# An mLSTM kernel with a feed-forward block: first weight quarter loaded first and converted between the first two cells, no warm-up matmuls, k scaled where v was

## The chip, the core and the metric

The kernel runs on one core of a Trainium2 chip. Its time is the device time of one execution in microseconds (us); the figure before the change is the median of three executions. The profile is that of one further execution. Engines are named as in the profile: PE (matrix engine; PEld is its loading of stationary operands), DVE (vector engine), ACT (scalar engine), POOL (GpSimd), SP (the sync engine, which here only issues DMAs). An engine's name with a q behind it, as SPq or ACTq, is its instruction queue, where DMAs are issued.

## The reference

Two blocks follow one another. The first is an mLSTM cell over 4 batches x 8 heads, 768 time steps, head dimension 40. The second takes its output as 3072 tokens of 320 features through a feed-forward block of width 2048 with a leaky ReLU.

```
for t in range(S):
    m_new = max(f[t] + m, i[t])
    f_stab, i_stab = exp(f[t] + m - m_new), exp(i[t] - m_new)
    C = f_stab * C + i_stab * outer(v[t], k[t])
    n = f_stab * n + i_stab * k[t]
    denom = max(|n . q[t]|, 1)
    y[t] = sigmoid(o[t]) * (C @ q[t]) / denom
x = y as (4*768, 320)
h = x @ w_in                       # 320 x 2048
out = max(0.01 * h, h) @ w_out     # 2048 x 320
```

q, k, v and the gates are 4-byte floats. The two weight matrices arrive as 8-byte floats and are made into 4-byte floats inside the kernel.

## The kernel before

**Chunks and cells.** Time is cut into NB = 6 chunks of 128 steps. A cell is one chunk of one batch, with all 8 heads: 24 cells, numbered s = 4c + b. Inside a cell the recurrence is written as products: scores k·q, a weight matrix from the gates, values from weights and v, and a state handed to the next chunk. Chunk 0 has no state before it and is handled by code of its own; later chunks work on two halves of 64 steps.

**Gates.** `gates(c)` makes running sums and maxima of the gates on DVE, `gates_exp(c)` their exponentials on ACT, `gates_T(c)` transposes them on PE (the result, `gT`, is copied by DVE). For c = 0 the gates lie in `f0` and `i0`, tiles of 128 rows that hold RG copies of the 32 (batch, head) rows. For c > 0, `gates_exp` also writes two results to DRAM (`a_dr`), from where SP spreads them over partitions (`spread`, `spread_q`).

**A cell of chunk 0.** `spread_mask(s)` (L411) puts a causal mask into PSUM with PE, `spread_first(s)` (L422) adds gate sums to it with narrow matmuls, `prep_exp` (L439) takes eight exponentials on ACT into the tile `w`. `u_transpose` (L514, L517) transposes k and q on PE and copies them to `kqT` on ACT. `u_scores` (L526) makes k·q on PE and multiplies it into `w` on DVE (L530). `prep_vu` (L449, L453) multiplies v with a gate on POOL. `u_state` (L538, L546) makes the state from k and that scaled v. `u_values` (L613) multiplies `w` with v. `prep_o` and `gate` (L467, L604 to L628) apply the output gate on ACT, DVE and POOL, and `u_x` (L719 to L724) transposes the cell's result into `xT`, the input of the feed-forward block.

**A cell of a later chunk.** `prep_mask` (L430) adds the mask on POOL, `prep_state` scales the state on POOL (L558) and calls `prep_vu`, which here scales v half by half in two POOL operations (L460). `u_parts` makes scores (L584) and the state's increment (L589) on PE, DVE multiplies and adds (L594, L562), `prep_kq` scales q on DVE (L486). `u_plain` (chunk 1) or `u_mix` (later ones) makes the outputs. `prepare_step(n)` fills constant parts of the state tile of slot n with three memsets on POOL (L156 to L158); there are NL = 4 slots.

**Weights.** `w_in` comes in QN = 4 quarters of 512 columns. `load_weights(n)` issues a quarter as ten DMAs of 128 KB, 64 partitions each (L213); `w_out` comes in 8 pieces of one DMA (L218). `narrow_weights(n)` is a Python generator of seven steps that converts one piece from 8 to 4 bytes: an Abs on ACT (L231), then six operations on DVE (L233, L237, L241, L243, L245, L247). Each call of `next` puts one step into the program at that place. A quarter's steps work on 128 x 1280 elements.

**Feed-forward.** `ff_units(0)` gives the units of chunk 0: each of the first 16 is a half unit, 20 records on PE (L734) followed by two leaky ReLUs on ACT (L742); the rest are the second product (L769). Later chunks have units of their own. A cell's output of chunk c is fed to the feed-forward units of chunk c while the cells of chunk c + 1 run.

**What sets the order.** PE, DVE, ACT and POOL run in the order in which the Python program emits their instructions (`manual_schedule`). For the first chunk this order is written out by hand in `first_chunk`. After it comes a loop over c: for c = 1 it goes through the remaining 30 feed-forward units of chunk 0, emits some steps of weight conversion before each (`run(now, ...)`), and puts in a cell's part wherever `place` says (the list holds a unit number for each of 13 parts). SP's queue is ordered by the tile framework and runs in order as well; a DMA on SP or ACT waits for the one that used the same of 8 completion semaphores before.

**Buffers.** The masks of a cell, and each feed-forward unit, take two of the four PSUM buffers of the pool `psf`; transposes, scores, values and states share four of the pool `psc`.

Of the kernel before, what the change touches and what calls it, by code (L numbers as in the profile page):

```python
# [9 lines left out]
F32 = mybir.dt.float32  # L10
# [3 lines left out]
ALU = mybir.AluOpType  # L14
# [4 lines left out]
def kernel(  # L19
# [58 lines left out]
    dr = ctx.enter_context(tc.tile_pool(name="dr", bufs=1, space=bass.MemoryType.DRAM))  # L78


    RG = P // BH
    f_all = f_gate.rearrange("b h s -> (b h) s")
    i_all = i_gate.rearrange("b h s -> (b h) s")
    f0 = gp.tile([P, P], F32, name="f0")
# [5 lines left out]

    def load_fi(c):
        t = fi[c] = wk.tile([BH, 2, P], F32, name="fi")
        eng = nc.scalar if c < 3 else nc.sync
        eng.dma_start(t[:, 0, :], f_all[:, ts(c, P)])
        eng.dma_start(t[:, 1, :], i_all[:, ts(c, P)])

    load_fi(1)
    load_fi(2)

    ident = consts.tile([P, P], F32, name="ident")  # L100
    make_identity(nc, ident[:])
# [86 lines left out]
    def load_weights(n):  # L188

        m = n - QN  # L190
        if n < QN:
            dst = w_in[:, n, :]
        else:
            dst = w_out[:, 2 * m : 2 * m + 2, :].rearrange("p a d -> p (a d)")
        to = dst
        if wide:
            if n < 2:
                at = NF * GT - 2 * WC * (n + 1)
                raw = acts_l[:, at : at + 2 * WC].bitcast(U64)
            elif n < QN:  # L200
                raw = raw_t[:, WC * (n - 2) : WC * (n - 1)]
            elif m < 2:
                raw = w_out[:].rearrange("p f d -> p (f d)")[:, (2 + m) * WC : (3 + m) * WC].bitcast(U64)
            else:
                at = (4, 0, 1, 2, 3, 4)[m - 2] * HW
                raw = raw_t[:, at : at + HW]
            raws[n] = (raw, dst)
            to = raw
        if n < QN:
            src = moe_w_in[:, n * QC : (n + 1) * QC].rearrange("(k p) (r c) -> r p k c", p=DP, r=2)  # L210
            for slot in range(KC):
                for r in range(2):
                    nc.sync.dma_start(  # L213
                        to[DP * r : DP * (r + 1), 2 * P * slot : 2 * P * (slot + 1)], src[r, :, SLOTS[r][slot], :],
                    )
        else:
            rows = moe_w_out[2 * m * P : 2 * (m + 1) * P, :]
            nc.sync.dma_start(to.rearrange("p (a d) -> p a d", d=Dm), rows.rearrange("(a p) d -> p a d", p=P))  # L218
# [37 lines left out]
    def gates(c):  # L256


        m0 = m0s.get(c)
        n = P if c == 0 else BH  # L260
        fc, il = (f0[:], i0[:]) if c == 0 else (fi[c][:, 0, :], fi[c][:, 1, :])
        F = wk.tile([n, P], F32, name="F", bufs=1)
        nc.vector.tensor_tensor_scan(F[:], fc, zeros[:n].to_broadcast([n, P]), 0.0, op0=ALU.add, op1=ALU.add)
        if c > 0:
            il_t = wk.tile([BH, P], F32, name="il", bufs=1)
            nc.vector.tensor_scalar(il_t[:], il, scalar1=m0[:], scalar2=None, op0=ALU.subtract)
            il = il_t[:]
        m = wk.tile([n, P], F32, name="m", bufs=1)
        nc.vector.tensor_tensor_scan(m[:], fc, il, -1e30 if c == 0 else 0.0, op0=ALU.add, op1=ALU.max)
        a = f0 if c == 0 else wk.tile([n, P], F32, name="a", bufs=1)  # L270
        nc.vector.tensor_tensor(a[:], F[:], m[:], op=ALU.subtract)
        bu = wk.tile([BH, 3, P], F32, name="bu", bufs=1)
        nc.vector.tensor_tensor(bu[:, 0, :], il[:BH], F[:BH], op=ALU.subtract)
        if c + 1 < NB:
            m1 = wk.tile([BH, 1], F32, name="m0")
            if c == 0:
                nc.vector.tensor_copy(m1[:], m[:BH, P - 1 :])
            else:
                nc.vector.tensor_tensor(m1[:], m0[:], m[:, P - 1 :], op=ALU.add)
            m0s[c + 1] = m1  # L280
        if c > 0:
            na = wk.tile([BH, 1], F32, name="na")
            nc.vector.tensor_tensor(na[:], m[:, SL - 1 : SL], F[:, SL - 1 : SL], op=ALU.subtract)
        bus[c] = bu, a, (na if c > 0 else None)
# [156 lines left out]
    def prep_vu(s):  # L441

        c, b = divmod(s, B)
        d = st[s]
        if s < NS:
            d["vu"] = wk.tile([P, H, 2, V1], F32, name="vu")
            g = gT[c][:, 1, ts(b, H)].unsqueeze(2).unsqueeze(3)
            if c == 0:
                nc.gpsimd.tensor_tensor(  # L449
                    d["vu"][:, :, :, :DB], d["va"][:, :, :D].rearrange("p h (k d) -> p h k d", d=DB),  # L450
                    g.to_broadcast([P, H, 2, DB]), op=ALU.mult,
                )
                nc.gpsimd.tensor_tensor(  # L453
                    d["vu"][:, :, :, DB], d["va"][:, :, D : D + 2], gT[c][:, 1, ts(b, H)].unsqueeze(2).to_broadcast([P, H, 2]),
                    op=ALU.mult,
                )
            else:
                for u in range(2 if c + 1 < NB else 1):
                    rows = ts(u, SL)
                    nc.gpsimd.tensor_tensor(  # L460
                        d["vu"][rows], S_v[s % NL][rows, u, :, :, :V1], g[rows].to_broadcast([SL, H, 2, V1]), op=ALU.mult,
                    )

    def prep_o(s):

# [104 lines left out]
    def u_parts(s):  # L570
# [11 lines left out]
        for h in range(H):  # L582
            for u, toks, rows in subs(s):
                nc.tensor.matmul(  # L584
                    bank[1 - u][toks, h, :], lhsT=kqT[rows, 0, ts(h, SL)], rhs=kqT[rows, 1, ts(h, SL)], start=True, stop=True,
                )
            for u, toks, rows in subs(s):
                if u < ends:
                    nc.tensor.matmul(  # L589
                        dC[u][:, h].rearrange("p k d -> p (k d)"), lhsT=d["k"][toks, h, :D],  # L590
                        rhs=d["vu"][toks, h].rearrange("p k d -> p (k d)"), start=True, stop=True,
                    )
        for u, toks, rows in subs(s):
            nc.vector.tensor_tensor(mixed(s)[toks, u], w[toks], bank[1 - u][toks], op=ALU.mult)  # L594
# [208 lines left out]
    def run(steps, n=None):  # L803

        for _ in range(H if n is None else n):
            next(steps, None)
# [18 lines left out]

    def first_chunk():

        load(0)
        load(1)
        load_o(0)  # L830
        load_o(1)
        load_weights(0)
        load(2)
        load(3)
        load_o(2)
        load_o(3)
        gates(0)
        gates_exp(0)
        warm(6)
        spread_mask(0)  # L840
        spread_mask(1)
        u_transpose(0)
        bu, a, _ = bus[0]
        gates_T(0, bu)
        spread_first(0, a)
        run(prep_exp(0))
        spread_first(1, a)
        prep_vu(0)
        prep_vu(1)
        prepare_tiles()  # L850
        u_transpose(1)
        u_scores(0)
        u_state(0)
        run(prep_exp(1))
        gates(1)
        gates_exp(1)
        load_weights(1)
        u_scores(1)
        u_values(0)
        u_state(1)  # L860
        spread_mask(2)
        spread_first(2, a)
        prep_o(0)
        gate(0)
        prep_o(1)
        spread_mask(3)
        spread_first(3, a)
        u_values(1)
        gate(1)
        w = narrow_weights(0)  # L870
        for _ in range(2):
            next(w, None)
        u_x(0)
        u_transpose(2)
        run(prep_exp(2))
        prep_vu(2)
        u_x(1)
        for _ in w:
            pass
        u_transpose(3)  # L880
        prep_vu(3)
        u_scores(2)
        u_state(2)
        run(prep_exp(3))
        prepare_step(0)
        prepare_step(1)
        ffs = ff_units(0)
        ffs[0]()
        ffs[1]()
        u_scores(3)  # L890
        u_values(2)
        u_state(3)
        prep_o(2)
        gate(2)
        w = narrow_weights(1)
        next(w, None)
        u_gates(1)
        u_values(3)
        prep_o(3)
        gate(3)  # L900
        u_x(2)
        for _ in w:
            pass
        u_x(3)
        prepare_step(2)
        prepare_step(3)
        return ffs

    E = mybir.EngineType
    with tc.manual_schedule(engines={E.PE, E.DVE, E.Activation, E.Pool}):  # L910
# [12 lines left out]

        ffs = ffs[2:]
        fetch = {4: (3, 4), 8: (5, 6), 13: (7,)}
        place = (5, 7, 9, 11, 11, 13, 15, 17, 20, 21, 23, 25, 27)
        now = (None for n in range(2, QN + NF // 2) for _ in narrow_weights(n))
        for c in range(1, NB + 1):
            if c > 1:
# [5 lines left out]
            for i in range(n_ff):  # L935
                if c == 1:
                    run(now, 2 if i < 10 else 3 if i < 14 else 4)
                    for n in fetch.get(i, ()):
                        load_weights(QN + n)
                    if i == 3:  # L940
                        prep_mask(B)
                        prep_state(B)
                        ahead(B)
                        load_fi(3)
# [59 lines left out]
```

## Time and profile before

| | us |
|---|---|
| median of 3 executions | 543.99 (543.73 to 547.78) |
| the profiled execution | 544.61 |
| its span in the trace | 542.8 |
| PE busy | 523.8 (97%) |
| DVE busy | 245.2 (45%) |
| ACT busy | 156.5 (29%) |
| POOL busy | 127.5 (23%) |

The largest groups of PE are the two products of the feed-forward block: L734 219.9 us and L769 215.1 us. The page's chain of waits, followed back from the last instruction, is PE for 81% of the span, DVE for 9%, SP's queue for 5%. Busy shares are means over the whole span; the page also cuts the span into 40 slices of 13.6 us and gives each engine's busy share in each slice as a digit of tenths. The row PEclk is the clock that PE was granted, in tenths of full speed. In the timeline the first two numbers of a row are start and length in us; brackets at the end hold the idle time before the first instruction of the row, and what ended it. A matmul of 4-byte floats shows as two records.

### The profile page before, as it was taken

To read this page: it belongs to the slowest core of one execution; us is meant where nothing else is said; L and a number is where in the kernel's file an instruction comes from. 1 tells how busy PE (TensorE), PEld (TensorE's weight loads), DVE (VectorE), ACT (ScalarE), POOL (GpSimd) and SP (SyncE) were. 2 spreads that over 40 slices of the span, in tenths; PEclk is the share of its full clock that TensorE was granted. 3 is DMA by queue.
4 is the path that set the end of the run, shared out by engine and by line. 5 is a ranking of instruction groups with operands and counts; after the bars stand their busy time and mean duration, and the time that the engine had idled before them with its cause. 6 is when DMAs were issued, how large, how long until landed. Compare 5 with 4: busy or idle time off the path is not lost.

```text
span 542.8 us, 11533 instructions
## 1 busy us (share of the span) xinstructions
PE 523.8 (97%) x4572; PEld 335.7 (62%) x4572; DVE 245.2 (45%) x423; ACT 156.5 (29%) x426; POOL 127.5 (23%) x157
## 2 busy tenths in 40 slices
PE   8978887989999999999999999999999999999997
PEld 7768776756745567645477644577654577644675
DVE  2659999999326445235536135525035532000000
ACT  4544735442233312034221034320043400022100
POOL 4346424351203332203332103323002200000000
PEclk9978999998999999999999999999999999999999
DMA  9967787876424655554556645555532121100000
GB/s 127 168 177 168 167 187 202 190 170 146 105 55 111 132 129 124 156 111 105 127 138 131 145 104 108 121 141 139 134 98 57 45 83 35 46 0 1 12 13 24
DMA packets 166005, 60.21 MB, mean 111 GB/s; under 512 B 129024, under 2 KB 156224, under 8 KB 165952
## 3 DMA queue, kind: packets, MB, share of 16 engines
q1 hardware_dynamic: 165568, 59.35, 48.4%
q8 instruction: 36, 0.59, 0.5%
q10 hardware_dynamic: 384, 0.13, 0.1%
q14 instruction: 17, 0.14, 0.1%
HBM read 52.72 MB, written 6.72 MB: 110 GB/s over the span
## 4 chain that ended last, share of the span: by engine, by line
PE 81%; DVE 9%; SPq 5%; DMA 2%; issue 1%; ACT 0%; POOL 0%; DVEq 0%; ACTq 0%; POOLq 0%
PE po L769 36%; PE ph L734 33%; PE pT L669 3%; SPq L213 3%; PE sd L584 2%; DVE qn L486 2%; PE ab L411 1%; PE xt L719 1%; DVE w_out L241 1%; PE ab L422 1%; PE sd L589 1%; DVE raw L243 1%; DVE w_out L247 1%; DMA ea<-a_dr 1%; DMA rb<-in_q_dram 1%
## 5 line engine op out<-in xcount | busy, mean ns | idle before, releaser
L734 PE MATMUL ph<-xT,w_in 64*128 64x512 f32 (+1 forms) x1120 | 219.9, 543 | 5.0 <-ACT acts L742 2.5
L769 PE MATMUL po<-w_out,acts 128*128 128x320 f32 x768 | 215.1, 438 | 0.0
L769 PEld LDWEIGHTS po<-w_out,acts 128*128 128x128 f32 x768 | 144.7, 191 | 60.9 <-issue 3.4
L734 PEld LDWEIGHTS ph<-xT,w_in 64*128 64x128 f32 x1120 | 109.6, 192 | 96.1 <-issue 84.6
L742 ACT ACTIVATE acts<-ph 128x512 f32<-128x512 f32 (+1 forms) x112 | 53.8, 532 | 144.1 <-PE ph L734 143.9
L594 DVE TENSOR_TENSOR qn<-w,sd 64x512 f32<-64x512 f32 x40 | 27.4, 685 | 128.9 <-PE sd L589 93.9
L558 POOL TENSOR_TENSOR S<-S,f 40x336 f32<-40x336 f32 x36 | 32.1, 892 | 188.1 <-PE pT L669 142.1
L439 ACT ACTIVATE w<-w,gT 128x64 f32<-128x64 f32 x160 | 42.5, 339 | 16.8 <-POOL w L430 16.7
L460 POOL TENSOR_TENSOR vu<-S,gT 64x336 f32<-64x336 f32 x36 | 31.4, 872 | 5.2 <-DMA S<-in_v_dram 2.6
L683 POOL TENSOR_TENSOR xb<-xb,den 128x320 f32<-128x320 f32 x16 | 11.6, 727 | 87.3 <-DVE xb L680 87.3
L486 DVE TENSOR_TENSOR qn<-kqT,ea 64x512 f32<-64x512 f32 (+1 forms) x40 | 31.4, 784 | 1.3
L777 ACT COPY hn<-po 128x320 f32<-128x320 f32 x12 | 5.1, 426 | 87.7 <-PE po L769 87.7
L777 ACT COPY y<-po 128x320 f32<-128x320 f32 x12 | 5.1, 426 | 83.1 <-PE po L769 83.1
L676 DVE STREAM_TRANSPOSE hb<-pT 128x512 f32<-128x512 f32 x16 | 11.5, 717 | 37.7 <-PE pT L669 37.7
L430 POOL TENSOR_TENSOR w<-w,i 128x512 f32<-128x512 f32 x20 | 28.0, 1398 | 1.0
L584 PEld LDWEIGHTS sd<-kqT 40*64 40x64 f32 x640 | 20.2, 134 | 12.3 <-issue 10.1
L584 PE MATMUL sd<-kqT 40*64 40x64 f32 x640 | 23.0, 221 | 0.0
L669 PEld LDWEIGHTS pT<-qn,S 128*64 128x64 f32 x512 | 16.2, 138 | 10.5 <-issue 6.9
L687 DVE STREAM_TRANSPOSE x<-xb 128x512 f32<-128x512 f32 x16 | 17.6, 1101 | 7.7 <-POOL xb L683 7.7
L480 DVE STREAM_TRANSPOSE kqT<-rb 128x512 f32<-128x512 f32 x32 | 20.7, 681 | 0.0
L589 PE MATMUL sd<-vu,kn 64*40 64x42 f32 x576 | 20.4, 214 | 0.0
L562 DVE TENSOR_TENSOR S<-S,sd 40x336 f32<-40x336 f32 x36 | 18.1, 503 | 0.9
(118 smaller groups left out, 361.3 us busy)
## 6 DMA issues: line engine op xcount, KB each, us to landing
w<-a_dr SPq DMA_DIRECT2D x40, 128.0 KB
ea<-a_dr SPq DMA_DIRECT2D x40, 128.0 KB
rb<-in_k_dram SPq DMA_DIRECT2D x64, 80.0 KB
rb<-in_q_dram SPq DMA_DIRECT2D x64, 80.0 KB
rb<-in_o_gate_dram SPq DMA_DIRECT2D x64, 80.0 KB
kn<-in_k_dram SPq DMA_DIRECT2D x24, 160.0 KB
raw<-in_moe_w_out_dram SPq DMA_DIRECT2D x6, 640.0 KB
S<-in_v_dram SPq DMA_DIRECT2D x80, 40.0 KB
```

The lines of the kernel that those rows point to most:

```text
L430: nc.gpsimd.tensor_tensor(w, w, cm2.unsqueeze(1).to_broadcast([P, H, SL]), op=ALU.add)
L439: yield nc.scalar.activation(w[:, h, :], of, AF.Exp, bias=gT[c][:, 0, bh : bh + 1], scale=1.0)
L460: nc.gpsimd.tensor_tensor(d["vu"][rows], S_v[s % NL][rows, u, :, :, :V1], g[rows].to_broadcast([SL, H, 2, V1]), op=ALU.mult,)
L486: nc.vector.tensor_tensor(mixed(s)[rows, 1 - r], d["kqT"][rows, 1].rearrange("p (h t) -> p h t", t=SL), d["ea"][rows], op=ALU.mult,)
L558: nc.gpsimd.tensor_tensor(new, old, g, op=ALU.mult)
L584: nc.tensor.matmul(bank[1 - u][toks, h, :], lhsT=kqT[rows, 0, ts(h, SL)], rhs=kqT[rows, 1, ts(h, SL)], start=True, stop=True,)
L589: nc.tensor.matmul(dC[u][:, h].rearrange("p k d -> p (k d)"), lhsT=d["k"][toks, h, :D], rhs=d["vu"][toks, h].rearrange("p k d -> p (k d)") ...
L594: nc.vector.tensor_tensor(mixed(s)[toks, u], w[toks], bank[1 - u][toks], op=ALU.mult)
L669: nc.tensor.matmul(pT[DP * r : DP * (r + 1), j * P + u * SL : j * P + (u + 1) * SL], lhsT=S[:, u, h, :], rhs=m[:, u, h, :], start=True, st ...
L734: nc.tensor.matmul(ph[r][:, cols], lhsT=w_row(r, slot, j), rhs=xT[DP * r : DP * (r + 1), slot, cols], start=(slot == 0), stop=(slot == KC ...
L742: nc.scalar.activation(acts[:, f, cols], ph[r][:, cols], AF.Prelu, alpha=0.01)
L769: nc.tensor.matmul(po[n][:], lhsT=acts[:, f, ts(n, P)], rhs=w_out[:, f, :], start=(f == 0), stop=(f == NF - 1),)
```

## The change

- **Gates of chunk 0.** RG goes from 4 to 2: `f0` and `i0` are loaded in two copies of 32 rows, two DMAs each, and `gates(0)` works on 64 rows instead of 128.
- **Gate loads of chunks 1 and 2** (`load_fi`) move from ACT's queue at the start to SP's queue: chunk 1 behind the loads of cell 0, chunk 2 behind the second weight quarter.
- **Weight quarters.** `load_weights(0)` is the first call of `first_chunk`, ahead of k, q and v of cell 0, and half of its ten DMAs are issued by ACT. `load_weights(1)` follows the first chunk's loads at once.
- **Warm-up matmuls** (`warm(6)`, L305) are gone; the masks of cells 0 and 1 are PE's first work.
- **Order of the first chunk.** Abs and the first three DVE steps of quarter 0 stand ahead of the exponentials of cell 0, the fourth step between cells 0 and 1, the rest behind the gate of cell 1. Transposes of cell 0 move behind `gates_T`. Masks of cells 2 and 3 move behind `u_x(0)`, `gates(1)` and `gates_exp(1)` too. The first feed-forward unit follows the transposes of cell 3, the second the gate of cell 2. All four `prepare_step` come last.
- **k instead of v is scaled in chunks 1 to 5.** One POOL operation of 128 x 320 per cell replaces two of 64 x 336; the matmul of L589 takes scaled k as its stationary operand and v straight from the state tile.
- **The loop of c = 1.** The first cell's parts come one feed-forward unit later, `place` and the test on i.

```diff
-    RG = P // BH
+    RG = 2
     def load_fi(c):
         t = fi[c] = wk.tile([BH, 2, P], F32, name="fi")
-        eng = nc.scalar if c < 3 else nc.sync
-        eng.dma_start(t[:, 0, :], f_all[:, ts(c, P)])
-        eng.dma_start(t[:, 1, :], i_all[:, ts(c, P)])
-
-    load_fi(1)
-    load_fi(2)
+        nc.sync.dma_start(t[:, 0, :], f_all[:, ts(c, P)])
+        nc.sync.dma_start(t[:, 1, :], i_all[:, ts(c, P)])
...
                 for r in range(2):
-                    nc.sync.dma_start(
+                    eng = nc.scalar if n == 0 and r == 1 else nc.sync
+                    eng.dma_start(
...
-        n = P if c == 0 else BH
-        fc, il = (f0[:], i0[:]) if c == 0 else (fi[c][:, 0, :], fi[c][:, 1, :])
+        n = RG * BH if c == 0 else BH
+        fc, il = (f0[:n], i0[:n]) if c == 0 else (fi[c][:, 0, :], fi[c][:, 1, :])
...
-                for u in range(2 if c + 1 < NB else 1):
-                    rows = ts(u, SL)
-                    nc.gpsimd.tensor_tensor(
-                        d["vu"][rows], S_v[s % NL][rows, u, :, :, :V1], g[rows].to_broadcast([SL, H, 2, V1]), op=ALU.mult,
-                    )
+                d["ku"] = d["vu"][:].rearrange("p h k d -> p (h k d)")[:, : H * D].rearrange("p (h d) -> p h d", d=D)
+                nc.gpsimd.tensor_tensor(
+                    d["ku"], d["k"][:, :, :D], gT[c][:, 1, ts(b, H)].unsqueeze(2).to_broadcast([P, H, D]), op=ALU.mult,
+                )
...
-                        dC[u][:, h].rearrange("p k d -> p (k d)"), lhsT=d["k"][toks, h, :D],
-                        rhs=d["vu"][toks, h].rearrange("p k d -> p (k d)"), start=True, stop=True,
+                        dC[u][:, h].rearrange("p k d -> p (k d)"), lhsT=d["ku"][toks, h],
+                        rhs=S_v[s % NL][toks, u, h, :, :V1], start=True, stop=True,
...
     def first_chunk():
+        def give(steps, n=H):
+            for _ in range(n):
+                next(steps, None)
+
+        load_weights(0)
         load(0)
+        load_fi(1)
         load(1)
         load_o(0)
         load_o(1)
-        load_weights(0)
         load(2)
         load(3)
         load_o(2)
         load_o(3)
+        load_weights(1)
+        load_fi(2)
         gates(0)
         gates_exp(0)
-        warm(6)
         spread_mask(0)
         spread_mask(1)
-        u_transpose(0)
         bu, a, _ = bus[0]
         gates_T(0, bu)
         spread_first(0, a)
+        spread_first(1, a)
+        w0, w1 = narrow_weights(0), narrow_weights(1)
+        give(w0, 4)
         run(prep_exp(0))
-        spread_first(1, a)
+        u_transpose(0)
         prep_vu(0)
         prep_vu(1)
         prepare_tiles()
-        u_transpose(1)
         u_scores(0)
         u_state(0)
         run(prep_exp(1))
-        gates(1)
-        gates_exp(1)
-        load_weights(1)
+        u_transpose(1)
+        give(w0, 1)
+        u_values(0)
         u_scores(1)
-        u_values(0)
+        prep_o(0)
+        gate(0)
         u_state(1)
+        u_values(1)
+        prep_o(1)
+        gate(1)
+        give(w0)
+        u_x(0)
         spread_mask(2)
         spread_first(2, a)
-        prep_o(0)
-        gate(0)
-        prep_o(1)
         spread_mask(3)
         spread_first(3, a)
-        u_values(1)
-        gate(1)
-        w = narrow_weights(0)
-        for _ in range(2):
-            next(w, None)
-        u_x(0)
+        gates(1)
+        u_x(1)
+        gates_exp(1)
         u_transpose(2)
         run(prep_exp(2))
         prep_vu(2)
-        u_x(1)
-        for _ in w:
-            pass
-        u_transpose(3)
-        prep_vu(3)
         u_scores(2)
         u_state(2)
+        u_transpose(3)
         run(prep_exp(3))
-        prepare_step(0)
-        prepare_step(1)
+        prep_vu(3)
         ffs = ff_units(0)
         ffs[0]()
-        ffs[1]()
         u_scores(3)
         u_values(2)
         u_state(3)
         prep_o(2)
         gate(2)
-        w = narrow_weights(1)
-        next(w, None)
-        u_gates(1)
+        ffs[1]()
+        give(w1, 1)
         u_values(3)
         prep_o(3)
         gate(3)
         u_x(2)
-        for _ in w:
-            pass
+        give(w1)
+        u_gates(1)
         u_x(3)
-        prepare_step(2)
-        prepare_step(3)
+        for n in range(NL):
+            prepare_step(n)
         return ffs
...
-        place = (5, 7, 9, 11, 11, 13, 15, 17, 20, 21, 23, 25, 27)
+        place = (6, 8, 10, 11, 12, 13, 15, 17, 20, 21, 23, 25, 27)
...
-                    if i == 3:
+                    if i == 4:
                         prep_mask(B)
```

More of the change, by code (lines that the diff above doesn't have):

```diff
@@ L269, in gates @@
         nc.vector.tensor_tensor_scan(m[:], fc, il, -1e30 if c == 0 else 0.0, op0=ALU.add, op1=ALU.max)
-        a = f0 if c == 0 else wk.tile([n, P], F32, name="a", bufs=1)
+        a = f0[:n] if c == 0 else wk.tile([n, P], F32, name="a", bufs=1)
         nc.vector.tensor_tensor(a[:], F[:], m[:], op=ALU.subtract)
```

## The prediction

> **What bounds the kernel now.** I read the page's slices first: which engine is full, and when.
>
> ```profile
> PE   8978887989999999999999999999999999999997
> DVE  2659999999326445235536135525035532000000
> PEclk9978999998999999999999999999999999999999
> ```
>
> A slice is 13.6 us. From the tenth on PE is at 9 and nothing but PE work counts there. Before it DVE stands at 9 (slices 4 to 10) and PE has holes: the first 150 us are the only place where time can be won. Then the busy time by stage (us of the stage, busy per engine in the order PE, PEld, DVE, ACT, POOL, then granted clock, DMA share, GB/s):
>
> ```profile
> 28.00:32.00 4.00, 1.93 (x34) 1.52 (x32) 3.90 (x4) 4.00 (x14) 3.89 (x6) 0.97 0.51 149
> 32.00:39.00 7.00, 6.24 (x32) 5.07 (x34) 2.56 (x5) 0.76 (x3) 1.34 (x4) 0.53 0.61 186
> 45.00:50.00 5.00, 4.33 (x42) 4.09 (x44) 4.86 (x7) 1.65 (x5) 4.34 (x8) 0.66 0.64 137
> 50.00:62.00 12.00, 12.00 (x164) 10.20 (x162) 11.79 (x14) 6.14 (x11) 9.41 (x7) 1.00 0.78 162
> 90.00:93.00 3.00, 0.12 (x2) 0.15 (x3) 2.87 (x8) 2.10 (x4) 0.12 (x1) 1.00 1.11 346
> ```
>
> PE idles 2.07 us in 28 to 32, and after that gap the clock is halved: 0.53 for 7 us, again 0.66 in 45 to 50. From 45 on DVE is 97% full. So there are two stages: a prologue (0 to 49) in which PE's own work and two halvings count, and a stage (45 to 110) paced by DVE. The timeline, in order of time, has the joints:
>
> ```profile
> 1.47 2.93 PE L305 MATMUL warm<-ident 128*128 128x128 f32 x12 [1.47 <-POOL ident masks.py:199]
> 20.29 1.38 ACT L231 ACTIVATE w_in<-acts 128x1280 f32<-128x1280 f32 x1 [2.02 <-DMA acts<-in_moe_w_in_dram]
> 31.21 1.49 DVE L247 TENSOR_TENSOR w_in<-w_in,acts 128x1280 f32<-128x1280 f32 x1
> 32.76 7.44 PE L734 MATMUL ph<-xT,w_in 64*128 64x256 f32 x40 [2.07 <-DVE w_in L247]
> 45.31 0.82 DVE L233 TENSOR_SCALAR w_in<-w_in 128x1280 f32<-128x1280 f32 x1
> ```
>
> The first quarter lands at 20.29, is converted by 32.7, and the first feed-forward units wait 2.1 us for it; DVE takes up the second quarter at 45.31, behind the gate of cell 3, and is full from there. 45.31 is the number to watch.
>
> **What the Trainium skill says.** "TensorE: Matmul & The Clock Gate", section "What's actually happening": TensorE's clock is halved by default and after idle windows of about 3.4 us, and released by busy ones. The trace agrees: 0.53 after the gap at 31. "SBUF — State Buffer", section "SBUF: two separate sides": DVE and GpSimd share a port pair, held for a whole instruction, so that a DVE operation with two SBUF inputs and a GpSimd operation that reads SBUF block one another. The trace agrees; the same DVE operation beside POOL's scaling of v and without:
>
> ```profile
> 54.49 2.54 POOL L460 TENSOR_TENSOR vu<-S,gT 64x336 f32<-64x336 f32 x2
> 56.44 1.94 DVE L241 SCALAR_TENSOR_TENSOR w_in<-raw,w_in 128x1280 uint32<-128x1280 uint32 x1
> 68.20 1.49 DVE L241 SCALAR_TENSOR_TENSOR w_in<-raw,w_in 128x1280 uint32<-128x1280 uint32 x1
> ```
>
> "DMA: Bandwidth & Descriptors", section "Issuing engines are not separate DMA queues": a second issuing engine saves issue time only. Here issue is what costs: SP needed 7.25 us for the ten pieces of the first quarter (0.72 each).
>
> **The change part by part.**
>
> *Warm-up out.* 12 records, 2.93 us. Each took 0.244 us; the same 128x128 shape in L514 takes 0.11 (8 in 0.88), so they ran at half rate. Now the masks (8 records, 3.52 us in the chain) start at about 1.7 and run the first 2.7 us at half rate: 1.35 us of work done, 2.2 left, end 6.5 instead of 7.9. Gain 1.4 here; if the release came one window of 3.4 us later, 1.7 is lost instead.
>
> *Two gate copies instead of four; gate loads of chunks 1 and 2 to SP.* Four issues of 0.45 fewer at the start, four on ACT moved to SP, behind v of cell 0 and behind the second quarter. Nothing on the path: in their place ACT issues five weight pieces, 5 x 0.6, until 4.7 to 5.2 (4.72 before), then table load 1.28 and Exp 0.40 as before: 6.5 to 6.9 against 6.45.
>
> *First quarter first, on two queues.* Five issues on each, done by 5.2; the last piece was usable 2.8 us after its issue ended (17.52 to 20.29), so 7.6 to 8.0. Abs 1.38 stands on ACT ahead of the exponentials of cell 0: they start at 9.0 to 9.4 (10.04 before): hidden. SP brings k, q, v of cell 0 only from 5.2 on (2.58 before) with 1.3 MB ahead of them: I put q at 9.6, bounds 8.5 and 11. PE meanwhile has masks (6.5), transposed gates (7.2) and 32 spread records (1.93 us) to 9.2.
>
> *New order of the cells.* The copy of kqT of cell 0 now follows Abs and 8 exponentials: 9.0 + 2.2 + 1.1 = 12.3, so the scores start at 12.3 (11.85 before) and PE idles about 2.5 us between 9.2 and 12.3. Masks 2 and 3 (1.91 + 1.09, twice: 6.0 us) filled PE at 16.3 to 22.3; now they come after u_x(0), so cells 0 and 1 run as a chain: scores 13.4, product on DVE 1.28 (14.6), values 15.8, scores 1 16.9, product 18.2, values 1 19.3, gate 0 about 1.0 plus POOL 0.72 (20.0), u_x(0) 21.2, masks to 27.2, u_x(1) 28.4. The quarter is done on DVE at about 24.4 (32.7 before): the 2.07 us wait of L734 is gone. What is late next: ACT. Behind u_x(1) stand its copies 0.86, four gate exponentials 1.2 (at 16.6 before, off the path) and kqT of cell 2 1.1: scores 2 at 31.5, PE idle about 2 us. Transposes of cell 3 wait for DVE's product of cell 2 (34.4), one feed-forward unit 2.25 (20 of the 0.1125 us records), scores, values and state of 2 and 3, the second unit: values 3 end at 43.1, gate 3 at 44.2. Against 45.3: **-1.1 at full clock**. The gap at 29.5 to 31.5 is like the one at 30.7 to 32.8, so I expect the halving again, now on scores 2, state 2 and transposes 3: 1.5 us of work doubled, half of it under the wait for exponentials: **+0.7**.
>
> *Second quarter.* Its conversion stays behind gate 3 on DVE: it moves with it, -0.4. FF units of that quarter then wait for DVE (8.5 us, as 45.31 to 53.79).
>
> *SP.* Five of the first ten issues leave SP (3.6 us), and the second quarter goes ahead of chunk 1's a_dr writes. a_dr waits for gates(1) (30 instead of 26.5) with the third quarter's pieces behind it; the fourth quarter starts about 45 instead of 49.01. ACT waited 1.81 us for it at 58.99; PE's wait after it (1.91) sits in a stage that DVE paces: between 0 and -1.9, I take 0.
>
> *k scaled in place of v.* Two POOL operations of 64x336 per cell become one of 128x320, as L449 (0.72 alone). The pair costs DVE the lock: the pair at 96.53 (2.21) lay over L237, L241, L243 in 2.79 us that take 1.81 alone (0.48, 0.83, 0.50, rows at 102.98 to 104.35). Half of 0.98 back per cell, 5 cells while DVE is full: 5 x 0.45 = **-2.2**; bounds 0 and -2.5. On PE the shapes stay (64x40 weights, 42 columns), with a strided right side like L639's: 0. After 150 PE hides POOL.
>
> *All four prepare steps last, cells one unit later.* Each step is 0.25 + 0.25 + 0.52 on POOL; two stood at 31.2, now all 4.1 us precede the mask of cell 4. L241 beside such memsets took 1.49 (47.43), as alone: 0. In cells one unit later, PE has feed-forward work to cover: 0, bounds -1 and +1.
>
> Sum: -1.1 + 0.7 - 2.2 = -2.6 on the profiled execution (544.61, span 542.8), which is 0.62 above the median: 541.4 against 543.99.
>
> **The rivals.** *Early halving (slower).* PE is only about 60% busy with small matmuls in 7.9 to 11.3. In 42 to 45.4 it was busy some 70% and was halved; in 62 to 66, with 58% of feed-forward work, it was not. If halved at 11.3 until 18, scores 0, state 0, transposes 1 and values 0 (1.09 + 0.44 + 0.95 + 1.06 = 3.5) double; 0.7 is slack: +2.8. With the second halving a window longer (+0.9) and the DVE relief at its half (+1.1): -2.6 + 4.8, **546.2**. It decides once gate 3 ends beyond 47.5, 2.2 later than now. *More is freed.* With the fourth quarter earlier, PE's holes of 50 to 100 (7.2 us: 1.91 in 62 to 64, 1.42 in 72 to 74, 1.01 in 74 to 90, 2.88 in 90 to 93) close by about half: **538**. Against it: DVE has no hole there. *Nothing passes.* DVE's pace swallows the POOL relief and the prologue ends where it did: **544**.
>
> **How the numbers follow.** Forecast 0.50, early halving 0.25, more freed 0.13, nothing 0.12. 1% is 5.4 us, about what a measurement of this kernel can tell from no change, so most cases lie within. Forecast's own range 539 to 543.5. The 8 in 10 takes half of "more freed", and early halving up to a late release of the masks as well (546.2 + 1.7, and 0.6 for late q): 537 to 548.5. Faster by over 1% (under 538.6): 0.15; slower (over 549.4), both delays together with q at its bound: 0.14; within: 0.71.
>
> **What would show it.** Right: masks end near 6.5; L231's first Abs at 7.6 to 8; the quarter's last step before 25; no wait of L734 for w_in in the first unit; gate 3's end and the next L233 at 44 to 46; L241 nearer 1.49. Wrong: a clock near 0.5 between 11 and 18, L233 of the second quarter beyond 47.5, DVE no longer full in 50 to 110, or a wait of POOL's k scaling for DMA.

## The result and the profile after

| | before | after |
|---|---|---|
| median, us | 544.59 (542.76 to 548.14, 20 runs) | 547.38 (546.04 to 549.51, 20 runs) |
| ratio | | 1.005, interval 1.0031 to 1.0068 |
| span of the profiled execution, us | 542.8 | 545.5 |
| DVE's first step of the second quarter, us | 45.31 | 49.48 |
| DVE's last step of weight conversion, us | 135.32 | 137.69 |
| POOL busy, us | 127.5 | 109.3 |

The change costs 0.5%. The ratios leave out executions more than 1.5% above the fastest of the same kernel; only the kernel with the loads alone, further down, had such, four of eight, at a lower granted clock. The page's slices of the changed kernel:

```profile
PE   6888988988999999999999999999999999999997
DVE  4746999999416454226435135525035432000000
PEclk9789999998999999999999999999999999999999
```

From the eleventh slice on PE is at 9 (before: from the tenth). The loss lies in the first slices: PE starts at 6 where it had 8, and DVE is full from the fifth slice instead of the fourth. The timeline of the changed kernel shows the joints (its line numbers are up to four lower than those of the kernel before):

```profile
1.71 5.81 PE L408 MATMUL ab<-cmask,ident 128*128 128x512 f32 x8 [1.71 <-POOL cmask L104]
...
9.79 1.36 ACT L228 ACTIVATE w_in<-acts 128x1280 f32<-128x1280 f32 x1 [2.50 <-DMA kn<-in_k_dram]
10.35 0.65 PE L510 MATMUL tkq<-ident,kn 128*128 128x128 f32 x4 [0.72 <-DMA kn<-in_k_dram]
...
11.05 2.15 ACT L436 ACTIVATE w<-ab,gT 128x128 f32<-128x128 f32 x8
...
11.55 0.66 PE L510 MATMUL tkq<-ident,qn 128*128 128x128 f32 x4 [0.55 <-DMA qn<-in_q_dram]
...
13.04 1.11 ACT L513 COPY kqT<-tkq 128x512 f32<-128x512 f32 x2
...
14.21 2.08 PE L522 MATMUL sc<-kqT 40*128 40x128 f32 x16 [2.00 <-ACT kqT L513]
...
35.53 1.16 PE L522 MATMUL sc<-kqT 40*128 40x128 f32 x16 [1.41 <-ACT kqT L513]
...
39.19 2.87 PE L730 MATMUL ph<-xT,w_in 64*128 64x256 f32 x20
...
49.48 0.82 DVE L230 TENSOR_SCALAR w_in<-w_in 128x1280 f32<-128x1280 f32 x1
```

The same timeline of the kernel before has two rows to compare, transposes of k and scores of cell 0:

```profile
7.76 0.60 PE L514 MATMUL tkq<-ident,kn 128*128 128x128 f32 x4
...
11.85 1.16 PE L526 MATMUL sc<-kqT 40*128 40x128 f32 x16
```

The last conversion step on DVE, after and then before:

```profile
137.69 0.98 DVE L244 TENSOR_TENSOR w_out<-w_out,raw 128x640 f32<-128x640 f32 x1
```

```profile
135.32 0.98 DVE L247 TENSOR_TENSOR w_out<-w_out,raw 128x640 f32<-128x640 f32 x1
```

PE waits for k of cell 0 to 10.35, then for q to 11.55, then for ACT's copies. What holds up the copies is ACT itself: the transposes of q are done at 12.2, but ACT is busy without a pause from 9.79, with Abs of the quarter, the exponentials of cell 0 and only then the copies. Abs reads the weights alone, so it waits to 9.79 for the last of them; the k in its bracket is an inference of the view, and PE has k only at 10.35. Scores 0 start at 14.21, 2.36 later than before, and take 2.08 where 1.16 is their length at full clock. The wait of the first feed-forward unit for its weights is gone (39.19 has no bracket). Busy time by stretch tells what happened to the clock. Of the changed kernel (stretch, its length, busy PE, PEld, DVE, ACT, POOL, then granted clock, DMA share, GB/s):

```profile
10.00:15.00 5.00, 2.10 (x14) 1.63 (x16) 3.66 (x3) 5.00 (x16) 2.15 (x2) 0.78 1.35 140
15.00:20.00 5.00, 5.00 (x65) 4.36 (x62) 2.93 (x5) 2.87 (x9) 2.22 (x7) 0.53 1.45 155
```

and of the kernel before:

```profile
10.00:15.00 5.00, 5.00 (x75) 4.24 (x72) 1.84 (x4) 4.96 (x18) 2.56 (x9) 1.00 1.21 193
15.00:20.00 5.00, 5.00 (x71) 3.35 (x71) 4.58 (x16) 1.95 (x8) 0.06 (x1) 1.00 0.74 192
```

PE idles 2.9 us between 10 and 15. The trace also records when the clock was halved and when it was released: here from 12.82 to 19.65. A halved clock leaves PE "full" with about half the work. Before, it was full at full clock in both stretches.

### The profile page after: what moved, and what is told of

It reads as the page before. It is cut to its first block, busy times and chain, and to the rows that moved or that the text cites. A ratio compares the mean times of both kernels' runs of the same rounds, so it can differ in the third digit from the quotient of the medians.

```text
span 545.5 us, 11438 instructions
## 1 busy us (share of the span) xinstructions
PE 522.6 (96%) x4560; PEld 332.6 (61%) x4560; DVE 241.7 (44%) x423; ACT 156.2 (29%) x426; POOL 109.3 (20%) x141
## 4 chain that ended last, share of the span: by engine, by line
PE 81%; DMA 6%; DVE 3%; SPq 2%; ACT 2%; issue 2%; POOL 2%; ACTq 0%; POOLq 0%; DVEq 0%
PE po L765 36%; PE ph L730 33%; PE pT L665 3%; PE sd L580 2%; DMA w<-a_dr 2%; PE xt L715 2%; DMA ea<-a_dr 1%; DMA w_out<-in_moe_w_out_dram 1%; SPq L338 1%; PE tkq L510 1%; DVE qn L482 1%; PE sc L522 1%; DMA acts<-in_moe_w_in_dram 1%; ACT w L436 1%; PE hN L635 1%
## 5 line engine op out<-in xcount | busy, mean ns | idle before, releaser
L730 PE MATMUL ph<-xT,w_in 64*128 64x512 f32 (+1 forms) x1120 | 216.8, 536 | 2.2 <-ACT acts L738 1.7
L730 PEld LDWEIGHTS ph<-xT,w_in 64*128 64x128 f32 x1120 | 106.9, 187 | 92.4 <-issue 84.6
L554 POOL TENSOR_TENSOR S<-S,f 40x336 f32<-40x336 f32 x36 | 30.9, 858 | 206.6 <-PE pT L665 153.1
L427 POOL TENSOR_TENSOR w<-w,i 128x512 f32<-128x512 f32 x20 | 26.8, 1340 | 0.1
L585 PE MATMUL sd<-S,vu 64*40 64x42 f32 x576 | 20.4, 214 | 0.0
L665 PE MATMUL pT<-qn,S 128*64 128x64 f32 x512 | 18.4, 225 | 0.0
```

Source lines behind the costliest of these rows:

```text
L427: nc.gpsimd.tensor_tensor(w, w, cm2.unsqueeze(1).to_broadcast([P, H, SL]), op=ALU.add)
L554: nc.gpsimd.tensor_tensor(new, old, g, op=ALU.mult)
L585: nc.tensor.matmul(dC[u][:, h].rearrange("p k d -> p (k d)"), lhsT=d["ku"][toks, h], rhs=S_v[s % NL][toks, u, h, :, :V1], start=True, stop ...
L665: nc.tensor.matmul(pT[DP * r : DP * (r + 1), j * P + u * SL : j * P + (u + 1) * SL], lhsT=S[:, u, h, :], rhs=m[:, u, h, :], start=True, st ...
L730: nc.tensor.matmul(ph[r][:, cols], lhsT=w_row(r, slot, j), rhs=xT[DP * r : DP * (r + 1), slot, cols], start=(slot == 0), stop=(slot == KC ...
```

## Experiments

Times are medians; ratios are to the kernel before. "Step" is DVE's first step of the second quarter (45.31 before, 49.48 after), from the profiled execution. It must be read with care. The changed kernel with v scaled as before, and with the old places in the loop, are the same program up to this step, and have it at 48.02 and 51.34; scaled k alone has 44.29 where the kernel before has 45.31. The clock was halved in other stretches there: with the old places from 14.75 to 28.41, for instance. So a shift of one or two microseconds in the step says something only where the trace shows what moved.

**k scaled alone, and all but that.** The first is the kernel before with only the scaling changed, the second the changed kernel with v scaled as before.

```diff
-                for u in range(2 if c + 1 < NB else 1):
-                    ... d["vu"][rows], S_v[s % NL][rows, u, :, :, :V1], ...
+                    d["ku"], d["k"][:, :, :D], gT[c][:, 1, ts(b, H)] ...
...
```

> The kernel before with one thing changed: from chunk 1 on k is scaled in one POOL operation, and v is read from the state tile. Theory (the new first chunk costs 4.2 us and the stage that DVE paces gives 1.8 back, because POOL holds the shared ports less): 1.5 to 2.5 us faster than before, DVE's second-quarter L233 stays at 45.3, and the last conversion step on DVE ends 1.5 to 2.5 us earlier than 135.3 + 1.0. Rival (what was given back came from the order of the loop or from the earlier fourth quarter, not from POOL): within 0.5 us of before.

> The changed kernel with v scaled in two POOL operations again, the rest as changed. Theory: 1.5 to 2.5 us slower than the changed kernel, so a ratio of 1.008 to 1.010 to before. Rival (the scaling does not matter): as the changed kernel, 1.005.

Measured: scaled k alone 543.41, 0.9969 (0.9951 to 0.9986); the changed kernel without it 549.52, 1.0094 (1.0075 to 1.0114), which is 2.1 above the changed kernel. So this part gains 1.4 us by the medians and 1.7 by the ratios in the first pair, 2.1 and 2.4 in the second, and the rest of the change costs about 4.9. The profile of scaled k alone does not show the gain where I had put it: from the step to the last conversion step it takes 90.0 us, as before (44.29 to 134.24), with a wait of ACT for the fourth quarter that has grown from 1.81 to 4.17. Where no such wait stands, in the changed kernel, the same stretch takes 88.2 with scaled k and 90.9 without, though the second execution also has two halvings in it that the first has not. So the gain rests on the times, and the way by which it reaches the end is shown only in part. In the changed kernel's timeline the lock between POOL and DVE is still there, but for one short instruction per cell:

```profile
59.52 1.18 POOL L456 TENSOR_TENSOR vu<-kn,gT 128x320 f32<-128x320 f32 x1
...
60.16 1.89 DVE L238 SCALAR_TENSOR_TENSOR w_in<-raw,w_in 128x1280 uint32<-128x1280 uint32 x1
...
70.09 1.49 DVE L238 SCALAR_TENSOR_TENSOR w_in<-raw,w_in 128x1280 uint32<-128x1280 uint32 x1
```

The DVE operation that overlaps POOL's scaling takes 1.89, the one without 1.49 (1.94 and 1.49 before); what shrank is POOL's time, from 9.0 us in eight operations (45 to 110) to 4.1 in four (50 to 110).

**The hole filled.** Idle matmuls, whose result nobody reads, around the transposes of cell 0:

```diff
         run(prep_exp(0))
+        warm(3)
         u_transpose(0)
+        warm(8)
```

> The changed kernel with idle matmuls in the two holes that PE has around the transposes of cell 0: three between the spread and the transposes, eight between the transposes and the scores (11 x 0.22 us at full clock, into a buffer of the other PSUM pool). Theory (the halved clock from 12.8 to 19.7 is a cost of its own): PEclk stays at 1.0 in 10 to 20, the scores of cell 1 start 1.5 to 2.5 us earlier than 20.25, the second quarter's first DVE step falls from 49.5 to 47 to 48, and the kernel is 1.5 to 2.5 us faster than the changed one, ratio about 1.001. Rival (the chain of waits through ACT and DVE is the limit, the clock is hidden under it): under 0.7 us gained.

Measured: 545.98, 1.003 (1.0016 to 1.0044). The timeline of this kernel:

```profile
12.28 1.95 PE L307 MATMUL warm<-ident 128*128 128x128 f32 x16
...
14.16 1.16 PE L527 MATMUL sc<-kqT 40*128 40x128 f32 x16
...
47.04 0.82 DVE L230 TENSOR_SCALAR w_in<-w_in 128x1280 f32<-128x1280 f32 x1
```

Scores 0 start no earlier (14.16), but take 1.16 instead of 2.08: the clock stays full from 7.07 to 34.37, and the step comes 2.4 earlier. The only thing altered is PE's idleness ahead of scores 0, so 2.4 of the 4.2 is the halved clock. Chance is an unlikely rival: in the seven kernels of this document that start with the weights, keep Abs ahead of the exponentials and fill no hole, the changed one among them, a halving began between 11.8 and 14.8; in the two with idle matmuls none began before 22.5. Of the 2.4, 1.1 (by the ratios) to 1.4 (by the medians) reach the end of the kernel; the intervals of the two ratios overlap, so this size is loosely known. The Trainium skill's "TensorE: Matmul & The Clock Gate", section "What's actually happening", gives an idle window of about 3.4 us as what halves the clock. The pair agrees that idleness is the cause, but the window need not be idle throughout: PE was busy for 1.53 of the 3.41 us ahead of 12.82.

**Abs behind the cell's own work; the exponentials of chunk 1's gates earlier; both with the hole filled.** In the first, Abs of quarter 0 stands behind the exponentials and transposes of cell 0, and DVE's first three steps later; in the second, `gates_exp(1)` stands before `u_x(1)`.

```diff
-        give(w0, 4)
         run(prep_exp(0))
         u_transpose(0)
+        give(w0, 1)
...
+        gates_exp(1)
         u_x(1)
-        gates_exp(1)
```

> The changed kernel with the conversion's Abs of quarter 0 behind the exponentials and the transposes' copies of cell 0 on ACT, and its DVE steps behind the products of cell 0. Theory (Abs waits for the weights and holds back cell 0's exponentials, 9.8 instead of 11.05): scores of cell 0 start at 12.9 to 13.3 instead of 14.2 (q lands for PE at 11.55), the second quarter's first DVE step at 48 to 48.7 instead of 49.5, 0.8 to 1.3 us faster than the changed kernel. Rival (q of cell 0, late behind the weights, sets the scores anyway): within 0.4 us of the changed kernel.

> The changed kernel with the four gate exponentials of chunk 1 ahead of the copies of cell 1's output on ACT. Theory (these 0.9 us stand on the path between u_x(1) and the scores of cell 2): the scores of cell 2 start at 34.6 instead of 35.5, the second quarter's first DVE step 0.5 to 0.9 us earlier, time 0.3 to 0.9 us less than the changed kernel. Rival (hidden): no difference.

> The changed kernel with idle matmuls in the first holes (3 and 4), Abs of quarter 0 behind cell 0's exponentials, and chunk 1's gate exponentials earlier. Theory (halved clock 2.4 us and late exponentials 2.0 us of the first chunk are separate costs): the second quarter's first DVE step at 44.5 to 46 instead of 49.5, time 2.5 to 4 us less than the changed kernel, ratio 0.997 to 1.000. Rival (both removals shorten the same wait): step at 46.5 to 47.5, ratio about 1.002.

Measured: 546.69, 1.0036 (1.002 to 1.0052), step 47.51; 546.62, 1.004 (1.0023 to 1.0057), step 47.78; all three 546.2, 1.0029 (1.0014 to 1.0044), step 46.78. Alone each moves the step by 1.7 to 2.4, together by 2.7: they shorten in part the same stretch, and their gains must not be added; in time, too, all three gain no more than the filled hole alone (546.2 and 545.98). None brings back 544.6. With Abs moved, the exponentials start at 9.62 and scores 0 at 13.04 instead of 14.21, now behind q (its transposes start at 11.71). With the gate exponentials earlier, scores 2 start at 34.82 instead of 35.53; the rest of that step's 1.7 is a second halving that this execution did not have. In time these two kernels, 1.0036 and 1.004, do not differ from the changed kernel by more than the one with the old places in the loop does (1.0036, at the end of this section), so their gain at the end is not shown.

**The loads alone, on the kernel before.** RG 2, gate loads on SP, first quarter as first large transfer on two queues; the order of the cells stays.

```diff
+        load_weights(0)
         load(0)
+        load_fi(1)
         load(1)
         load_o(0)
         load_o(1)
-        load_weights(0)
...
```

> The kernel before with the loads alone as in the change: quarter 0 first on two queues, gate copies two instead of four, gate loads of chunks 1 and 2 on SP. Order of the first chunk, warm-up, scaled v and loop as before. Theory (late q of cell 0 and the hole that it makes in PE cost more than the quarter's early landing gives): PE waits some 3.5 us for k and q at 7.9 to 11.6, the clock is halved in 10 to 20, the second quarter's first DVE step at 47 to 49 instead of 45.3, the kernel 1.5 to 3.5 us slower than before, ratio 1.003 to 1.006. Rival (the loads are harmless, the new order of instructions is what costs): within 1 us of before, since the first feed-forward units no longer wait for the quarter.

Measured: 555.15 (547.86 to 559.37, 8 runs), ratio 1.0091 (1.005 to 1.0132). The profiled execution took 558.96, so I take from it only the wait: PE waits 2.3 us for k of cell 0, to 10.47, and 0.6 for q. The cost is above the 1.003 to 1.006 that I expected. This kernel scales v as before, so its like is the changed kernel without scaled k, 1.0094 (1.0075 to 1.0114). The loads alone cost as much as the loads and the rest of the change together. That the new order costs anything of its own is not shown, though the wide interval leaves room for about 2 us either way.

**Cell 0's data first again.** The kernel with Abs and gate exponentials moved, without idle matmuls, and with `load(0)` ahead of `load_weights(0)`, the transposes ahead of the exponentials.

```diff
-        load_weights(0)
         load(0)
+        load_weights(0)
...
```

> The changed kernel with k, q and v of cell 0 loaded ahead of the quarter (still on two queues), transposes of cell 0 and their copies ahead of its exponentials, Abs of the quarter behind them, and chunk 1's gate exponentials earlier; no idle matmuls. Theory (the weights ahead of cell 0's k and q are what opens the holes and halves the clock): no wait of PE for k or q of cell 0, scores of cell 0 at 11 to 12.5 instead of 14.2, at most one halving before 30, the second quarter's first DVE step at 44 to 45.5, ratio to before 0.995 to 0.999 with the relief from scaled k in it. Rival (the chain of cells 0 and 1 without masks 2 and 3 as filler is slow in any case): step at 47 to 49, ratio 1.002 to 1.004.

Measured: 547.65, 1.0054 (1.0031 to 1.0076), step 48.59. Its timeline:

```profile
11.78 1.16 PE L522 MATMUL sc<-kqT 40*128 40x128 f32 x16 [0.72 <-ACT kqT L513]
...
14.88 0.63 PE L510 MATMUL tkq<-ident,kn 128*128 128x128 f32 x4 [1.50 <-DMA kn<-in_k_dram]
```

Scores 0 are back at 11.78 (11.85 before the change), but now k of cell 1, behind the same bytes, comes at 14.88, and the clock is halved from 17.05 to 27.29. The hole has moved by one cell. My expectation that putting cell 0 first would bring the time back was wrong; the step, 48.59, lies where the rival had it (47 to 49). That rival, a chain of cells 0 and 1 that is slow with any loads, is not excluded by this run, since the late data of cell 1 stands in it too.

**Fewer issues, same bytes.** If SP's issue (five weight pieces until 4.98, k of cell 0 only at 6.62) made k late, four DMAs per quarter instead of ten would help. Tried on the kernel before with scaled k, and on the changed kernel:

```diff
-            for slot in range(KC):
-                for r in range(2):
-                    eng.dma_start(... 2 * P * slot : 2 * P * (slot + 1)], src[r, :, SLOTS[r][slot], :])
+            for r in range(2):
+                at = 0
+                while at < KC:
+                    k0, m2 = run_of(r, at)
+                    eng.dma_start(... "p (k c) -> p k c", k=m2), src[r, :, k0 : k0 + 2 * m2 - 1 : 2, :])
+                    at += m2
```

> The kernel before with scaled k, and each quarter of w_in loaded by four DMAs (three or two slots of 256 columns each) instead of ten of one slot, same bytes. Theory (SP issues DMAs without a pause until 57, and ACT waits 4.2 us at 60.2 for the fourth quarter, which stands at the end of that queue): the fourth quarter's Abs at 53 to 57 instead of 60.2, PE's wait of 4.25 us before 65.1 falls under 1.5 us, ratio to before 0.991 to 0.995 (scaled k alone 0.997). Rival (DVE paces the stage and PE's waits there cost nothing): within 0.7 us of scaled k alone.

> The changed kernel with each quarter of w_in in four DMAs of 2 or 3 pieces instead of ten of one; the bytes and their order stay. If SP's issue of five pieces and the wait for one of eight completion semaphores made k and q of cell 0 late, k is issued near 3 to 4 us (6.62 before), transposes of cell 0 start at 8.5 to 9.5 (10.35), DVE's first step of the second quarter at 46.5 to 48 (49.48), and the time is 542 to 544 with what the later quarters bring. If the bytes ahead of k and q (1.3 MB) or the order of the cells decide, transposes stay at 10 or later, the step at 48.5 to 50, and only the later quarters gain, as much as in the kernel before: 547.4 less 2.5, 544.5 to 545.5.

Measured: on the kernel before with scaled k 540.92, 0.9938 (0.9917 to 0.996); on the changed kernel 548.37, 1.0069 (1.0041 to 1.0098). SP's queue and PE in the changed kernel with merged pieces:

```profile
3.06 0.59 SPq L337 DMA_DIRECT2D kn<-in_k_dram  x1
...
11.80 0.66 PE L514 MATMUL tkq<-ident,kn 128*128 128x128 f32 x4 [1.89 <-DMA kn<-in_k_dram]
```

k is issued 3.6 us earlier than in the changed kernel and is there 1.45 later. So an earlier issue alone does not bring k earlier; it comes late with the quarter's 1.3 MB ahead of it, in ten pieces or in four. The theory of SP's issue falls for the prologue. On the kernel before, fewer issues seem to pay elsewhere. ACT's first Abs of the fourth quarter, with scaled k and then with merged pieces as well:

```profile
60.17 1.41 ACT L231 ACTIVATE w_in<-raw 128x1280 f32<-128x1280 f32 x1 [4.17 <-DMA raw<-in_moe_w_in_dram]
```

```profile
58.12 1.40 ACT L235 ACTIVATE w_in<-raw 128x1280 f32<-128x1280 f32 x1 [1.45 <-DMA raw<-in_moe_w_in_dram]
```

The wait shrinks by 2.7 us, and the last conversion step ends 1.5 earlier (132.74 against 134.24). That it is 0.3% faster than scaled k alone is likely but not certain, as the intervals of the two ratios overlap a little; and the profile with scaled k alone has a halving from 63.36 to 70.19 that the merged one lacks, so how much is the wait and how much the clock stays open. In the changed kernel no such wait exists at this place, and merging gains nothing: its last step is at 137.83 against 137.69. The merged version of the kernel before is the fastest of this study.

**The masks of cells 2 and 3 between cells 0 and 1 again,** in the changed kernel, and the same with merged pieces:

```diff
         run(prep_exp(1))
+        spread_mask(2)
+        spread_first(2, a)
         u_transpose(1)
...
         u_state(1)
+        spread_mask(3)
+        spread_first(3, a)
         u_values(1)
...
```

> The changed kernel with the masks of cells 2 and 3 (6.0 us of PE) between cells 0 and 1 again: that of cell 2 ahead of the transposes of cell 1, that of cell 3 ahead of values 1. If the chain of cells 0 and 1 without that work between is a cause of the late second quarter, its first step on DVE moves from 49.5 to 47 to 48.5 and the time to 545.5 to 546.5. If holes ahead of scores 0 are all of it, the masks only stand in the way of u_x(0): the step stays at 49 to 50.5 and the time at 547 to 548.

> Both edits together. If both causes hold, the step comes at 45 to 46.5 and the time is 541 to 543; if neither, the step stays at 48.5 to 50.5 and the time is 544.5 to 545.5, from the later quarters alone.

Measured: 551.39, 1.0124 (1.0083 to 1.0165), step 53.28; with merged pieces 551.81, 1.0133 (1.0098 to 1.0169). The opposite of what I expected of a cause. In their old place the masks delay `u_x(0)` from 24.54 to 29.19; the clock is again halved, from 13.62 to 20.44, so the first mask alone takes 3.76 for the 1.98 of full clock. ACT's work then bunches further on, and the clock is halved there too, from 37.51 to 44.34:

```profile
37.98 2.08 PE L522 MATMUL sc<-kqT 40*128 40x128 f32 x16 [3.23 <-ACT kqT L513]
```

So with the late scores, moving the masks behind `u_x(0)` saves; with early ones it wasn't tried by itself.

**Second quarter converted earlier,** on the kernel before with scaled k: its loads ahead of the gates of chunk 1, Abs and three DVE steps ahead of scores 3.

```diff
+        w = narrow_weights(1)
+        for _ in range(4):
+            next(w, None)
         u_scores(3)
...
```

> The kernel before with scaled k, and with quarter 1 loaded ahead of chunk 1's writes of gates and its Abs and first three DVE steps put ahead of the scores of cell 3, where DVE had been idle for 6.6 us. Theory (DVE paces 45 to 140): DVE's stage loses about 3.5 us of work, the last conversion step on DVE ends 2.5 to 3.5 us earlier than with scaled k alone (135.2), ratio to before 0.991 to 0.993. Rival (PE's own waits in that stage take over): under 1 us beyond scaled k alone, ratio 0.996.

Measured: 544.05, 0.999 (0.997 to 1.001), where 0.991 to 0.993 was expected. The first step comes at 42.13 (44.29 with scaled k alone), but the quarter is finished at 54.5 instead of 52.8, and PE waits 3.7 us for DVE's product at 46. What DVE takes up early, cell 3 pays for.

**Old place of the cells in the loop of c = 1:** `place` and i == 3 as before.

> The changed kernel with the loop of chunk 1 as before: cells one feed-forward unit earlier. Theory (DVE paces that stage and PE has work to cover): within 0.7 us of the changed kernel, ratio 1.004 to 1.006. Rival (later cells are part of what the change costs): 1 to 2 us faster than the changed kernel.

Measured: 547.11, 1.0036 (1.002 to 1.0052), against 547.38 with the new place. No difference that this shows.

## Why the prediction failed

The direction failed: 541.4 was forecast from 543.99, and the kernel became slower, 547.38 against 544.59. Two terms failed. The first stands under **"First quarter first, on two queues"**: "they start at 9.0 to 9.4 (10.04 before): hidden". Abs of the quarter was not hidden: the weights were usable at 9.79, not at "7.6 to 8.0", so the exponentials of cell 0 started at 11.05 and scores 0 at 14.21, not at 12.3. The second is the sum under **"New order of the cells"**, "-1.1 at full clock" and "+0.7": it counted the hole ahead of scores 0 as idle time alone, and the clock was halved behind it. Instead of -0.4 at the number to watch, +4.2 came: 49.48 where the sum has 44.9. These 4.6 us, as far as single executions can tell:

- *Late data, 1.9.* 14.21 against 12.3. With Abs out of the way scores 0 start at 13.04, so 1.2 is Abs with its late weights. The other 0.7 is q: "I put q at 9.6, bounds 8.5 and 11", and it came at 11.55. I reckoned from the time of issue (SP free at 5.2); issue at 6.62 was late too, but the merged pieces showed that an earlier issue doesn't help.
- *First halving, 2.4.* This is what the rival "early halving" named, at the place it named: halved "at 11.3 until 18" there, 12.82 to 19.65 in the trace; its point of decision, gate 3 beyond 47.5, was passed (the last step of gate 3 on DVE starts at 49.07). It sized the halving at +2.8; filling the hole showed 2.4. I gave it a quarter of the chance, though the same paragraph had the sign for it: small matmuls that fill PE to 60%. The late data enlarged the hole: PE worked 2.1 of the 5 us from 10 to 15. I had charged late data and halving to two cases. The rival's total, 546.2, is near the measured time partly by luck: it has no late scores in it, and a longer second halving and a halved relief that did not come.
- *Second halving, 0.3 more than its +0.7.* It fell on scores 2 to transposes 3, as forecast (36.72 to 40.13), behind an idle 1.41 of PE. From scores 2 to the step it takes 13.9 to 14.1 us in the three kernels with one halving of 3.41 us in this stretch (the changed one, the one with the hole filled, the one with Abs later), and 12.9 to 13.0 in the six without. So it costs 1.0. That it came was luck: behind the same idle 1.4 us it did not come with v scaled as before, with the old places, or with merged pieces.

One comparison of the prediction was misread: 62 to 66, "with 58% of feed-forward work", holds 2.09 us of PE's work in 4.00, 52%.

Right were: **k scaled in place of v**, -2.2, where the runs show -1.4 to -2.4; the wait of the feed-forward for its first weights, gone, although the quarter was converted at 28.7 and not at 24.4; `place`, 0; and in **SP** the fourth quarter at 0: ACT meets no wait for it at 60.12, and merged pieces move nothing in the changed kernel. Masks ended at 7.5 instead of 6.5: the clock was released at 6.00 and not at 4.4, between the two cases named there. The 0 for the prepare steps wasn't tried by itself.

The sum in other terms: +4.2 at the step, of which the stage behind it gives back 1.8 (last conversion step +2.4), and the span ends +2.7. How much of a shift at the step reaches the end differs: with the hole filled about half of 2.4, with the masks between the cells about all of the 3.8; as the step comes from one execution each, these shares are rough.

## What to carry to other kernels

A large transfer moved ahead of small ones that start the program is paid by whoever needs these: look for the first wait that it lengthens, and at the bytes ahead of it as well as at the time of issue. An instruction that waits for the large transfer holds back everything behind it on its own engine, as Abs did with the exponentials. A hole that a change opens in PE costs twice when small matmuls follow it, once as idle time and once as halved clock, so check the two together. A chain of small steps answers to several cures, but in part they cure the same microseconds: measure them together before adding them. And a time read from one trace moves with the clock: kernels whose program is the same up to an instruction reached it up to 3.3 us apart here.

## What was unexpected

- The clock's first release moves from execution to execution with the same start of the program on PE: 6.00 in the changed kernel, 4.96, 5.37, 7.07, 7.69 and 7.92 in kernels that differ from it only later. Halvings came in lengths of 3.41 us or multiples.
- The spread of one kernel's times goes with the clock granted over the whole span. In 126 executions of the kernel before, 66 at a mean clock of 0.987 had a median of 543.8, 34 at 0.981 one of 546.1. The profiled execution of the changed kernel had 0.987 and still took 547.31: how much of the span is halved is not all, and here the halving meets the first cells.
- k of cell 0, issued 3.6 us earlier behind fewer and larger pieces, was there later.
